# Block-transposed q features and 32x32 array tiles in the last stage of a linear-attention plus gMLP kernel

## The chip, the cores and the metric

The kernel runs on one core of one Trainium2 chip. The metric is the device time of one execution in microseconds; the kernel before takes 630.05 us, the median of three runs (629.80 to 630.59). A row of the profile names an engine: PE is TensorE's matmuls, PEld its weight loads, DVE VectorE, ACT ScalarE, POOL GpSimd, SP SyncE, which here only issues DMAs.

## What is computed

Both branches start from the same layer-normed input and are added to it (one batch, 2048 tokens, width 512, 32 heads of 16; gMLP width 1376, halved to 688):

```python
xn = layernorm(x)
# A: linear attention with learned features
q, k, v = split(xn @ wqkv)                          # per head: 2048 x 16
phi(t) = concat(softmax(t @ w_phi), softmax(-t @ w_phi))    # 32 features per head
kv = phi(k).T @ v                                   # per head 32 x 16
z  = sum_s phi(k)
o  = (phi(q) @ kv) / (phi(q) @ z + 1e-6)
A  = o @ wo
# B: gMLP
h = gelu(xn @ w_in);  z1, z2 = h[:, :688], layernorm(h[:, 688:])
g = w_sp @ z2 + b_sp[:, None]                       # over the 2048 tokens
B = (z1 * g) @ w_out
out = x + A + B
```

All tensors are fp32. Big products are done with operands split into a rounded part h and a remainder l (`fp32r`): `mm3` issues three matmuls, hh, hl, lh, at lines 55, 56 and 57. Other matmuls take plain fp32, and one of those stands as two records in the trace.

## The kernel before, in words

The 2048 tokens are 16 tiles of 128. The stages, in order of time:

1. To about 210 us: x is normed and transposed; per tile, v, k and q are projected, the features of k are summed into kv and z, the unnormalised features of q go to DRAM (`e_d`: 1024 exponentials and 64 reciprocals a token), z1 before its gelu too.
2. To about 282 us: the rest of z1; the gate weights' second half (`w2`, by `load_win`); z is broadcast (`make_zb`), kv is turned (`make_kvT`); the first spatial operands are prepared (`prep_a`); the features of q tiles 0 and 1 are finished by `q_fin` and stored to `e_d` again (lines 590 to 594); then z2 is projected, activated, normed and split into operands B for a Strassen-like product.
3. To 494 us: 32 steps of `products` for w_sp @ z2, two output tiles (a "pair") at a time in four steps; after each pair `drain` (lines 708 to 721) reads seven PSUM banks with VectorE, and `gate` forms u = z1 * g, which goes to DRAM in two 16-bit planes and comes back transposed by DMA.
4. The last stage, from 494 us: per pair of token tiles, u @ w_out (`project_u`, 17 matmuls of 512 columns a tile: five `mm3` and two for a rest of 48 rows), the attention, and o @ wo (`project_o`, 12 matmuls) accumulated into the same PSUM bank; VectorE adds x (line 944) and SP stores.

The attention of a pair before: `q_fin` (lines 490 to 501) finishes the features of a tile on VectorE: a product with z (L494), a sum per head half (L495), four small operations (L496 to L499), a scaling (L501). Then `attend_T` (line 887) transposes 16 blocks of 128x128 on TensorE against an identity and ScalarE copies them out of PSUM (L900) in four pieces; tiles from 6 on are first copied by a GpSimd DMA (L872) into an `fp32r` tile, which makes the transposes `fp32r`. `attend` (line 904) issues 16 matmuls with 64 rows, 32 columns and 256 tokens:

```python
lasts[3] = pe.matmul(po[r][c * QP:(c + 1) * QP, j // NG], kvT[rows, j], fs[j // 2][rows, j % 2],
                     start=True, stop=True).ins
```

ScalarE rounds the result (L47) and VectorE forms its remainder (L51). For u, `gated` joins the two planes on ScalarE (L774), rounds (L47) and lets VectorE take the remainder (L51, 128x640).

Order: a planner of the framework sets each engine's order by a simulated timeline, but `tc.issue_after(x)` pins what follows behind x. Before, a few such pins (`fin`, `lasts`) order the last stage. DMA queues of SP and POOL are in order as well: an issue that waits holds what stands behind it. The PSUM banks of the last stage are two pools, `pst` (5 banks: transposes and attention) and then `pso` (3 banks: outputs), laid over the 8 banks of the spatial products.

The gate of the last pair of rows (tiles 14 and 15) is done late, in the last stage, after tile 9 (line 998).

Of the kernel before, what the change touches and what calls it, by code (L numbers as in the profile page):

```python
# [10 lines left out]
F32 = mybir.dt.float32  # L11
# [8 lines left out]
P = 128  # L20
S, D, H, DH, FH = 2048, 512, 32, 16, 688
NT = S // P
# [17 lines left out]
def mixer(ctx: ExitStack, tc: tile.TileContext, x, x_t, wv, wqkT, phi_bd, wo, w_in, wst, b_r, w_out, out):  # L40
# [449 lines left out]
    def q_fin(et, tmp, zb):  # L490

        e, r, t, w = et[:, :NF], *(et[:, NF + k * 2 * H:NF + (k + 1) * 2 * H] for k in range(3))
        den = et[:, NF + 6 * H:QW]
        dve.tensor_tensor(tmp, e, zb, op=ALU.mult)  # L494
        dve.tensor_reduce(t, heads(tmp), axis=AX.X, op=ALU.add)  # L495
# [5 lines left out]
        return e, dve.tensor_tensor(heads(e), heads(e), bc(w, 2 * H), op=ALU.mult).ins  # L501
# [45 lines left out]
    NE = 2  # L547
    with ExitStack() as p1:
# [27 lines left out]
        with ExitStack() as p1a:  # L576
            ta = p1a.enter_context(left("tmp1a", 1))
            for j in range(2):
                load_win(w2[j], 2 + j, ta)
# [9 lines left out]
        tb = p1.enter_context(left("tmp1b", 1))  # L589
        for s in range(NE):  # L590
            et = load_q(s, tb.tile([P, QW], F32, tag="et", bufs=2, name="et"))
            tmp = zw.tile([P, 4, FC], F32, tag="z2", bufs=2, name="qtmp").rearrange("p a b -> p (a b)")[:, :NF]
            e, _ = q_fin(et, tmp, zb)
            sp.dma_start(e_d[s, :, :NF], e)
# [131 lines left out]
    def gate(i, cb, z, planes):  # L726
        cb, first, _ = cb
        with tc.issue_after(first):
            act.activation(z[:, :, :FH], z[:, :, :FH], AF.Gelu_apprx_tanh)
# [6 lines left out]
        dve.tensor_copy(z[:, :, rm], rh.bitcast(F32))  # L736
        planes = planes.bitcast(U16).rearrange("p (k two n) -> p k two n", k=2, two=2)
        for k in range(2):
            act.activation(planes[:, k], halves(z[:, k]), AF.Copy)
# [52 lines left out]
    lasts, wu = [None] * 6, []  # L792

    def first_q(s):
        e = slot("eq", F32R)[:, :NF]
        sp.dma_start(e.bitcast(F32), e_d[s, :, :NF])
        return e
# [12 lines left out]
    g, es, ets = {}, {}, {}  # L810
    for n in range(NC):
# [4 lines left out]
        if n % NQ == NQ - 1 and i < NP - 1:  # L816
            c = gt.tile([P, 2 * UP], F32, tag="c", name="c")
            gate(i, drain(i, g, c[:, :2 * FH].rearrange("p (a b) -> p a b", a=4)), z, c)
# [9 lines left out]
        if n == NC - 3:  # L828
            zs = slot("zb", F32R)
            zb, ident_r = zs[:, :NF].bitcast(F32), zs[:, NF:NF + P]  # L830
            round_h(act, ident_r, ident)
# [3 lines left out]
            ets[2] = load_q(2, slot("et"))  # L835
            q2 = slot("qtmp")[:, :NF]
        if n == NC - 2:
            u1t = load_u(1, slot("u1").bitcast(U16)[:, :2 * UP])
            es[0], es[1] = first_q(0), first_q(1)
            ets[3] = load_q(3, slot("et"))  # L840
            wo_raw = []
            for c in range(ND):
                rows = [(r, r + QP) for r in range((c % 2 * NG * 2 + c // 2) * QP, D, 2 * QP)][:NG]
                t = ws.tile([P, QC, P], F32, tag=f"f{c // 2}", bufs=2, name="wof").rearrange("p a b -> p (a b)")
                with tc.issue_after(load_q.last):
                    wo_raw.append(load_part((sp, pool)[c % 2], wo, rows, t))
# [3 lines left out]
    with tc.issue_after(lasts[1]):  # L850
        es[2], last = q_fin(ets.pop(2), q2, zb)
    mid.close()

# [5 lines left out]
    fin = []  # L859

    def fetch_u(i):
        return load_u(i, cw.tile([P, 2 * UP], U16, tag="u", bufs=3, name="ut"))

    def features(s):
        with tc.issue_after(fin[-1]):
            es[s], ins = q_fin(ets.pop(s), slot("qtmp")[:, :NF], zb)
        fin.append(ins)
        if s < PLAIN:
            return
        e = es[s]  # L870
        es[s] = cw.tile([P, NF], F32R, tag="er", bufs=5, name="er")
        features.copied = pool.dma_start(es[s].bitcast(F32), e).ins  # L872

    def gated(t):
        u = joined(t, cw.tile([P, UP], F32, tag="uj", bufs=2, name="uj"))
        return gate_parts(u, wk.tile([P, KF * P], F32R, tag="uh", name="uh"),
                          wk.tile([P, KF * P], F32R, tag="ul", name="ul"), wk.tile([2 * REM, P], F32R, tag="rt", name="rt"))

    kvT = cw.tile([P, 2 * NG, QP], F32, name="kvT")
    us = {}  # L880
    ctx_psg.__exit__(None, None, None)
    fin.append(last)
    sp.dma_start(kvT.rearrange("p j b -> p (j b)"), kvT_d)
    pst = ctx.enter_context(psum("pst", 5))
    pso = ctx.enter_context(psum("pso", 3))

    def attend_T(s):

        fs = []
        for g in range(NG):  # L890
            pt = pst.tile([P, 2, 2, P], F32, tag="tr", name="ptq")
            for a in range(2):
                for k in range(2):
                    src = group(es[s + k], 2 * g + a)
                    if src.dtype == F32:
                        pe.transpose(pt[:, a, k], src, ident)
                    else:
                        pe.transpose(pt[:, a, k].bitcast(F32R), src, ident_r)  # L898
            f = wk.tile([P, 2, 2 * P], F32, tag="f", bufs=NG + 1, name="f")
            attend_T.last = act.activation(f, pt.rearrange("p a k b -> p a (k b)"), AF.Copy).ins  # L900
            fs.append(f)
        return fs

    def attend(fs):

        oT = [wk.tile([P, NG, 2 * P], F32R, tag=f"oT{k}", name="oT") for k in "hl"]
        po = [pst.tile([P, 2, 2 * P], F32, tag="tr", name="po") for _ in range(2)]
        for j in range(2 * NG):
            c = j % NG
            for r in range(2):  # L910
                rows = slice(r * HP, (r + 1) * HP)
                lasts[3] = pe.matmul(po[r][c * QP:(c + 1) * QP, j // NG], kvT[rows, j], fs[j // 2][rows, j % 2],  # L912
                                     start=True, stop=True).ins
        for k in range(2):
            gs = slice(2 * k, 2 * k + 2)
            lasts[5] = round_h(act, oT[0][:, gs], po[k])
            ins = rest_l(oT[1][:, gs], po[k], oT[0][:, gs])
        return oT, ins

    def project_u(i, u, between=None):  # L920
        uh, ul, rt = u
        parts = [(slice(0, D), pso.tile([P, D], F32, tag="out", name="pout"))]
        if i == NT - 1:
            more = pst.tile([P, 4, P], F32, tag="tr", name="pout2").rearrange("p a b -> p (a b)")
            parts = [(slice(k * D // 2, (k + 1) * D // 2), q[:, :D // 2]) for k, q in enumerate((parts[0][1], more))]
        order = ExitStack()
        for ds, p in parts:
            for c in range(KF):
                i_ = mm3(p, (uh[:, c], ul[:, c]), tuple(w[:, ds] for w in wu[c]), c == 0, False)
                if between and c == KF // 2:  # L930
                    order.enter_context(between(i_))
            for w in wu[KF]:
# [103 lines left out]
```

## Time and profile before

| what | value |
|---|---|
| median of three runs | 630.05 us (629.80 to 630.59) |
| span of the profiled execution, first to last instruction | 628.4 us |
| PE busy | 622.3 us |
| DVE busy | 505.3 us |
| ACT busy | 313.5 us |
| granted TensorE clock, mean | 1.000 |
| DMA, mean | 180 GB/s |

The span is that of one profiled execution; the page gives no other time of it, and the runs are timed separately. In a row of a timeline stand start, duration, engine, line, operation, output <- inputs, shape and count; in brackets the idle time before it and what ended it. In a row of a group stand busy time, mean duration in ns, and idle time. Matmuls overlap, so their durations add up to more than the time they take.

### The profile page before, as it was taken

To read this page: it belongs to the slowest core of one execution; us is meant where nothing else is said; L and a number is where in the kernel's file an instruction comes from. 1 tells how busy PE (TensorE), PEld (TensorE's weight loads), DVE (VectorE), ACT (ScalarE), POOL (GpSimd) and SP (SyncE) were. 2 spreads that over 40 slices of the span, in tenths; PEclk is the share of its full clock that TensorE was granted. 3 is DMA by queue.
4 is the path that set the end of the run, shared out by engine and by line. 5 is a ranking of instruction groups with operands and counts; after the bars stand their busy time and mean duration, and the time that the engine had idled before them with its cause. 6 is when DMAs were issued, how large, how long until landed. Compare 5 with 4: busy or idle time off the path is not lost.

```text
span 628.4 us, 11487 instructions
## 1 busy us (share of the span) xinstructions
PE 622.3 (99%) x4375; PEld 563.1 (90%) x4375; DVE 505.3 (80%) x925; ACT 313.5 (50%) x463; POOL 121.0 (19%) x213
## 2 busy tenths in 40 slices
PE   9999999999999999999999999999999999999997
PEld 6888888888888999999999999999999878877776
DVE  5979989998988579989987677786777789989721
ACT  5623333432343447788553654546445655557550
POOL 4552232222101004552010110101101200110100
PEclk9999999999999999999999999999999999999999
DMA  8467767555653861001467758667588966897921
GB/s 326 152 160 163 200 176 162 166 157 151 165 164 106 265 211 68 2 1 57 138 173 186 221 176 203 202 184 226 165 197 297 287 227 230 268 278 263 293 83 35
DMA packets 67091, 112.85 MB, mean 180 GB/s; under 512 B 30588, under 2 KB 32124, under 8 KB 67036
## 3 DMA queue, kind: packets, MB, share of 16 engines
q1 hardware_dynamic: 53036, 63.35, 34.8%
q0 software_dynamic: 11408, 42.61, 23.8%
q10 hardware_dynamic: 2592, 6.16, 2.6%
q8 instruction: 34, 0.56, 0.4%
q14 instruction: 21, 0.17, 0.1%
HBM read 60.69 MB, written 31.48 MB: 147 GB/s over the span
## 4 chain that ended last, share of the span: by engine, by line
PE 96%; DVE 3%; issue 0%; ACT 0%
PE g L57 11%; PE g L56 11%; PE g L55 11%; PE proj L55 6%; PE zps L55 6%; PE proj L57 6%; PE proj L56 6%; PE zps L57 6%; PE zps L56 6%; PE pout L55 6%; PE pout L56 5%; PE pout L57 5%; PE po L912 1%; PE kvps L322 1%; PE ptq L898 1%; PE pout L933 1%
## 5 line engine op out<-in xcount | busy, mean ns | idle before, releaser
L55 PE MATMUL g<-B,A 128*128 128x344 f32 x448 | 143.2, 320 | 0.0
L56 PE MATMUL g<-B,A 128*128 128x344 f32 x448 | 143.2, 320 | 0.0
L57 PE MATMUL g<-B,A 128*128 128x344 f32 x448 | 143.0, 320 | 0.0
L57 PEld LDWEIGHTS g<-B,A 128*128 128x128 f32 x448 | 84.1, 188 | 0.2 <-DVE A L51 0.2
L56 PEld LDWEIGHTS g<-B,A 128*128 128x128 f32 x448 | 84.2, 188 | 0.0
L55 PEld LDWEIGHTS g<-B,A 128*128 128x128 f32 x448 | 84.2, 188 | 0.0
L47 ACT ACTIVATE A<-S 128x512 fp32r<-128x512 f32 x64 | 39.4, 628 | 63.3 <-DVE S L538 40.4
L116 ACT ACTIVATE e<-e,r_x 128x1024 f32<-128x1024 f32 x32 | 36.7, 1148 | 46.0 <-DVE e L115 44.1
L51 DVE TENSOR_TENSOR A<-S,A 128x512 fp32r<-128x512 f32 x64 | 43.1, 684 | 9.7 <-ACT A L47 9.6
L55 PE MATMUL proj<-wqk_h,xT 128*128 128x512 f32 x124 | 49.6, 400 | 0.0
L57 PE MATMUL proj<-wqk_h,xT 128*128 128x512 f32 x124 | 48.8, 394 | 0.0
L56 PE MATMUL proj<-wqk_l,xT 128*128 128x512 f32 x124 | 48.7, 393 | 0.0
L118 DVE TENSOR_REDUCE sm<-e 128x64 f32<-128x1024 f32 x32 | 38.6, 1210 | 9.7 <-ACT e L116 9.5
L47 ACT ACTIVATE A<-wf 128x512 fp32r<-128x512 f32 x64 | 33.0, 516 | 19.4 <-PE g L57 8.7
L51 DVE TENSOR_TENSOR A<-wf,A 128x512 fp32r<-128x512 f32 x64 | 35.2, 549 | 9.2 <-ACT A L47 9.0
L55 PE MATMUL zps<-w_h,xT 128*128 128x344 f32 x128 | 41.8, 326 | 0.4 <-ACT z1f L146 0.3
L57 PE MATMUL zps<-w_h,xT 128*128 128x344 f32 x128 | 40.9, 319 | 0.0
L56 PE MATMUL zps<-w_l,xT 128*128 128x344 f32 x128 | 40.8, 319 | 0.0
L537 DVE TENSOR_TENSOR S<-wf 128x256 f32<-128x256 f32 x32 | 13.4, 420 | 27.1 <-DMA wf<-in_wst 27.1
L146 ACT ACTIVATE z1f<-zps,r_x 128x344 f32<-128x344 f32 (+1 forms) x30 | 17.0, 565 | 33.8 <-PE zps L57 33.3
L302 ACT ACTIVATE v<-proj,r_x 128x512 f32<-128x512 f32 x16 | 11.0, 685 | 44.2 <-PE proj L57 41.7
L900 ACT ACTIVATE f<-ptq 128x512 f32<-128x512 f32 x32 | 16.5, 604 | 26.7 <-PE ptq L898 16.8
(199 smaller groups left out, 1546.4 us busy)
## 6 DMA issues: line engine op xcount, KB each, us to landing
wf<-in_wst SPq DMA_DIRECT2D x64, 256.0 KB, 3.9
e_d<-e POOLq DMA_DIRECT2D x16, 544.0 KB, 3.7
et<-e_d SPq DMA_DIRECT2D x16, 544.0 KB, 5.5
zacc<-e POOLq DMA_DIRECT2D x16, 512.0 KB, 4.9
z_d<-z1f ACTq DMA_DIRECT2D x16, 344.0 KB, 3.8
z1t<-z_d POOLq DMA_DIRECT2D x16, 344.0 KB, 5.8
u_d<-c POOLq DMA_DIRECT2D x14, 384.0 KB, 2.7
er<-et POOLq DMA_DIRECT2D x10, 512.0 KB, 4.9
```

The source lines that it names most:

```text
L47: return act.activation(h, src, AF.Copy).ins
L51: return (eng or dve).tensor_tensor(l, src, h.bitcast(F32), op=ALU.subtract).ins
L55: pe.matmul(dst, ah, bh, start=start, stop=False)
L56: pe.matmul(dst, ah, bl, start=False, stop=False)
L57: return pe.matmul(dst, al, bh, start=False, stop=stop).ins
L116: softmax_pair.exp = act.activation(e, e, AF.Exp, scale=scale).ins
L118: dve.tensor_reduce(sm, heads(e), axis=AX.X, op=ALU.add)
L146: z1_raw.last = act.activation(z[:, k], p, AF.Copy, scale=r_x[:, s:s + 1]).ins
L302: ins = act.activation(v[s], proj(s, wv_h, wv_l, rest_last), AF.Copy, scale=r_x[:, s:s + 1]).ins
L322: ins = pe.matmul(kv_acc[k:k + QP, m // 4], vs[:, m * QP:(m + 1) * QP], e[:, m * HP:(m + 1) * HP], start=s == 0 and m < 4, stop=s == NT - ...
L537: dve.tensor_tensor(sums[:, 0], b[:, 0], b[:, 1], op=ALU.add)
L900: attend_T.last = act.activation(f, pt.rearrange("p a k b -> p a (k b)"), AF.Copy).ins
```

## The change

Four things, all around the attention:

- **Features.** `q_fin` is cut into `q_weigh` (L494, L495), `q_norm` (the rest) and a new `q_turn`: one VectorE block transpose of 128x1024, which transposes each 32x32 block in place of its own. 32 columns are just the features of one head, so a block comes out with features on partitions and 32 tokens in a row. TensorE's transposes, their ScalarE copies and the DMA copies to `fp32r` are gone.
- **Attention.** `attend` handles four token tiles at once: 128 matmuls, each with 32 rows (one block of 32 tokens' features), 32 columns and 4 x 32 tokens, over all sixteen 32x32 parts of the array; each of the four row groups has its own PSUM bank. `kv4` holds kvT four times, one copy per row group, loaded from DRAM.
- **Early features.** Three tiles instead of two, ahead of the second gelu stage, written before the first `prep_a`, their loads at the stage's start; they are stored turned.
- **u remainders.** From tile 4 on, ScalarE writes -h and a GpSimd DMA adds u to it; tiles 2 and 3 keep VectorE.

Besides: everything in the last stage is pinned in written order per engine (`in_line`); `pso` (4 banks) is allocated before `pst` (4 banks); wo is loaded in whole row blocks and earlier; the features of tile 3 are weighed ahead of the last `drain`; the late gate stands before the third attention. The core of the diff:

```diff
+    def q_turn(et, eT):
+        return dve.transpose(eT, et[:, :NF]).ins
...
-    NE = 2
+    NE = 3
...
+            tb = p1a.enter_context(left("tmp1b", 1))
             ta = p1a.enter_context(left("tmp1a", 1))
+            def early_q(s):
+                ets[s] = load_q(s, tb.tile([P, QW], F32, tag="et", bufs=2, name="et"))
+            def early_features(s):
+                tmp = tb.tile([P, NF], F32, tag="tq", name="tq")
+                q_weigh(ets[s], tmp, zb)
+                q_norm(ets[s])
+                q_turn(ets.pop(s), tmp)
+                sp.dma_start(e_d[s, :, :NF], tmp)
+            early_q(0)
+            early_q(1)
             for j in range(2):
                 load_win(w2[j], 2 + j, ta)
...
             raw[0], raw[1] = load_a(0), load_a(1)
+            early_features(0)
+            for s in range(2, NE):
+                early_q(s)
+            for s in range(1, NE):
+                early_features(s)
             A[0] = prep_a(0, raw.pop(0))
...
+            with tc.issue_after(lasts[1]):
+                weigh(NE)
...
+    pso = ctx.enter_context(psum("pso", 4))
+    pst = ctx.enter_context(psum("pst", 4))
+    QT = 4
...
+    def features(s):
+        weigh_next(s)
+        normed_q(s)
+        turn_q(s)
+    def gated(i, on_dve=False):
...
+            round_h(act, uh, u[:, full])
+            line["act"] = act.activation(rt, u[:2 * REM, KF * P:], AF.Copy).ins
+            if on_dve:
+                line["dve"] = rest_l(ul, u[:, full], uh)
+            else:
+                line["act"] = act.activation(ul, uh.bitcast(F32), AF.Copy, scale=-1.0).ins
+                line["pool"] = pool.dma_start(ul.bitcast(F32), u[:, full], accum_op=ALU.add).ins
+    def attend(k):
+        eg = egs.pop(k)
+        oT = [cw.tile([P, NG, QT, P], F32R, tag=f"oT{n}", name="oT") for n in "hl"]
+        po = [pst.tile([P, NG, QT, SQ], F32, tag="po", name="po") for _ in range(P // SQ)]
+        with in_line():
+            for g in range(NG):
+                for a in range(2):
+                    for c in range(P // SQ):
+                        for i in range(P // SQ):
+                            rows = slice(i * SQ, (i + 1) * SQ)
+                            h = 8 * g + 2 * c + a
+                            pi = pe.matmul(po[i][c * SQ:(c + 1) * SQ, g], kv4[rows, h % 4, h // 4],
+                                           eg[rows, :, h * SQ:(h + 1) * SQ], start=a == 0, stop=a == 1,
+                                           skip_group_check=True).ins
+            for i in range(P // SQ):
+                h, l = (t[:, :, :, i * SQ:(i + 1) * SQ] for t in oT)
+                ai = round_h(act, h, po[i])
+                vi = rest_l(l, po[i], h)
...
+    project_u(0)
+    fetch_u(3)
+    fetch_u(4)
+    normed_q(NE)
+    project_u(1)
+    gated(2, True)
+    turn_q(NE)
+    project_u(2)
...
+    for k in range(NT // QT):
+        b = k * QT
+        if k == 2:
+            with in_line():
+                gate(NP - 1, cb, z)
...
+        oT = attend(k)
+        project_u(b + 3)
+        if k == 2:
+            with in_line():
+                store_gated(NP - 1, z, gt.tile([P, 2 * UP], F32, tag="pl", name="pl"))
...
+            fetch_u(NT - 2)
+        for i in range(b, b + QT):
+            last = i == b + QT - 1
+            fetch_q(i + 6)
+            if i == 0:
+                turn_q(QT)
+            elif i + 4 < NT and not last:
+                features(i + 4)
+            if i + 4 < NT and not last:
+                gated(i + 4)
+            project_o(i, oT)
+            if last and i + 4 < NT:
+                features(i + 4)
+                project_u(b + 4)
+                gated(i + 4)
...
+        if k < NT // QT - 1:
+            weigh_next(b + 2 * QT)
+            project_u(b + 5)
+            project_u(b + 6)
```

So between two attentions TensorE does, in this order, the u projection of the fourth tile of the block, the o projections of its four tiles, and the u projections of the first three tiles of the next block; VectorE does the remainders of the attention, the features of the next four tiles (the first is weighed beforehand), and four output sums.

More of the change, by code (lines that the diff above doesn't have):

```diff
@@ L588, in mixer @@
         sp.dma_start(zb_d, zb)
[L589 to L594, printed above, removed]
     ctx_w1.__exit__(None, None, None)
@@ L849, in mixer @@
         uT.append(first_gate(u1t, wu_rest[1]))
-    with tc.issue_after(lasts[1]):
-        es[2], last = q_fin(ets.pop(2), q2, zb)
+    line.update(act=lasts[0], dve=lasts[1])
     mid.close()
@@ L885, in mixer @@
[L885 to L918, printed above, removed]
@@ L920, in project_u, with in_line @@
-    def project_u(i, u, between=None):
-        uh, ul, rt = u
+    ctx_psg.__exit__(None, None, None)
+    pso = ctx.enter_context(psum("pso", 4))
+    pst = ctx.enter_context(psum("pst", 4))
+    QT = 4
+    full = slice(0, KF * P)
+    us, egs, nxt, p = {}, {}, {0: uT[0], 1: uT[1]}, {}
+    wo_h, wo_l = (cw.tile([P, ND, D], F32R, name=f"wo{k}") for k in "hl")
+    def in_line():
+        order = ExitStack()
+        for ins in line.values():
+            order.enter_context(tc.issue_after(ins))
+        return order
@@ L927, in project_u @@
[L927 to L932, printed above, removed]
-                lasts[2] = pe.matmul(p, rt, w[:, ds], start=False, stop=False).ins
-        order.close()
-        return parts
-    def project_o(i, oT, parts):
-        ts = slice(i % 2 * P, (i % 2 + 1) * P)
-        xr = wk.tile([P, D], F32, tag="xr", bufs=3, name="xr")
-        sp.dma_start(xr, x[i * P:(i + 1) * P, :])
-        for ds, p in parts:
-            for c in range(ND):
-                lasts[4] = mm3(p, (oT[0][:, c, ts], oT[1][:, c, ts]), (wo_h[:, c, ds], wo_l[:, c, ds]), False, c == ND - 1)
-            dve.tensor_tensor(xr[:, ds], p, xr[:, ds], op=ALU.add)
-            sp.dma_start(out[i * P:(i + 1) * P, ds], xr[:, ds])
@@ new lines, in project_u, with project_o @@
+        with in_line():
+            for ds, q in parts:
+                for c in range(KF):
+                    mm3(q, (uh[:, c], ul[:, c]), tuple(w[:, ds] for w in wu[c]), c == 0, False)
+                for w in wu[KF]:
+                    ins = pe.matmul(q, rt, w[:, ds], start=False, stop=False).ins
+        line["pe"] = ins
+        p[i] = parts
+    def project_o(i, oT):
+        xr = wk.tile([P, D], F32, tag="xr", bufs=4, name="xr")
+        sp.dma_start(xr, x[i * P:(i + 1) * P, :])
+        for ds, q in p.pop(i):
+            with in_line():
+                for c in range(ND):
+                    pi = mm3(q, (oT[0][:, c, i % QT], oT[1][:, c, i % QT]), (wo_h[:, c, ds], wo_l[:, c, ds]),
+                             False, c == ND - 1)
+                line["dve"] = dve.tensor_tensor(xr[:, ds], q, xr[:, ds], op=ALU.add).ins
+            line["pe"] = pi
+            sp.dma_start(out[i * P:(i + 1) * P, ds], xr[:, ds])
@@ new lines, in mixer @@
+    with in_line():
+        for c in range(ND):
+            ai, vi = split_w(wo_raw[c], wo_h[:, c], wo_l[:, c])
+    line.update(act=ai, dve=vi)
+    fetch_u(2)
+    for s in range(NE):
+        sp.dma_start(turned(s), e_d[s, :, :NF])
+    project_u(0)
[6 more added lines that the diff above has]
+    project_u(2)
+    fetch_u(5)
+    fetch_q(QT + 1)
+    with in_line():
+        weigh(QT)
+    gated(3, True)
+    fetch_u(6)
+    normed_q(QT)
```

165 lines of the change are left out of this document (66 added, 99 removed).

## The prediction, made before the result

> **What bounds the kernel now.** I read the page's busy shares first, then its 40 slices, then its chain that ended last.
>
> ```profile
> PE 622.3 (99%) x4375; PEld 563.1 (90%) x4375; DVE 505.3 (80%) x925; ACT 313.5 (50%) x463; POOL 121.0 (19%) x213
> ...
> PE   9999999999999999999999999999999999999997
> ...
> PE 96%; DVE 3%; issue 0%; ACT 0%
> ```
>
> TensorE (PE) is busy from the first slice to the last but one, and the chain is 96% TensorE. So time is won only by taking instructions away from TensorE, or by closing one of its few holes. The change lives in the last stage, after the spatial products; the busy time by stretch shows who has room there:
>
> ```profile
> 495.30:593.60 98.30, 98.30 (x648) 77.65 (x648) 90.47 (x143) 57.08 (x80) 7.71 (x15) 1.00 0.81 255
> 593.60:625.50 31.90, 31.43 (x232) 25.84 (x230) 7.14 (x11) 11.11 (x18) 0.00 (x0) 1.00 0.27 87
> ```
>
> The columns are PE, weight loads, VectorE (DVE), ScalarE, GpSimd. VectorE is at 90.5 of 98.3 us until 593.6, then nearly idle:
>
> ```profile
> 591.15 1.23 DVE L501 TENSOR_TENSOR et<-et 128x1024 f32<-128x1024 f32 x1
> ```
>
> ```profile
> 608.64 1.48 PE L898 MATMUL ptq<-zb,er 128*128 128x128 f32 x16
> ```
>
> The last features are done at 592.4, 16 us before the last transposes take them. The change spends just this reserve. The TensorE timeline of one pair of token tiles gives the prices:
>
> ```profile
> 544.55 0.39 PE L57 MATMUL pout<-woh,oT 128*128 128x512 f32 x1
> 544.79 1.48 PE L898 MATMUL ptq<-zb,er 128*128 128x128 f32 x16
> 546.10 0.46 PE L55 MATMUL pout<-wu,uh 128*128 128x512 f32 x1
> 546.40 0.39 PE L56 MATMUL pout<-wu,uh 128*128 128x512 f32 x1
> ...
> 549.42 0.40 PE L57 MATMUL pout<-wu,ul 128*128 128x512 f32 x1
> 549.65 0.63 PE L933 MATMUL pout<-wu,rt 96*128 96x512 f32 x2
> 550.21 1.09 PE L912 MATMUL po<-f,kvT 64*32 64x256 f32 x32
> 551.24 0.50 PE L55 MATMUL pout<-wu,uh 128*128 128x512 f32 x1
> 551.57 0.39 PE L56 MATMUL pout<-wu,uh 128*128 128x512 f32 x1
> ```
>
> Matmuls are pipelined, so I price by start to start, not by duration: 549.42 to 549.65 is 0.23 us for a matmul of 512 columns. There is one hole, where the last stage begins:
>
> ```profile
> 494.18 0.32 PE L57 MATMUL g<-B,A 128*128 128x344 f32 x1
> 495.26 0.47 PE L55 MATMUL pout<-wu,uh_ul 128*128 128x512 f32 x1 [0.76 <-DVE c L712]
> ```
>
> **TensorE, removed.** Sixteen transposes per pair take 544.79 to 546.10, 1.31 us, and the matmul behind them needs 0.30 instead of 0.23: 1.38. The attention takes 550.21 to 551.24, 1.03 us; it starts 0.10 after the matmuls ahead of it would have made room (549.65 + 2 x 0.23), and the one behind it takes 0.33: 1.23. Together 2.61 us per pair, 20.9 for eight. Two pairs have transposes of the slower kind, and one attention waited for its evictions one by one:
>
> ```profile
> 528.47 1.91 PE L896 MATMUL ptq<-ident,et 128*128 128x128 f32 x16
> 517.15 1.88 PE L912 MATMUL po<-f,kvT 64*32 64x256 f32 x32
> ```
>
> That is 1.91 - 1.48 = 0.4 twice and 1.88 - 1.09 = 0.8, so 22.5 us go.
>
> **TensorE, added.** Four attentions, each of 4 x 2 x 4 x 4 = 128 matmuls with 32 rows, 32 columns and a moving part of 128. The old one is 16 matmuls in the program and 32 in the trace, so the new one is 256 records. Before, eight parts of the array shared 32 records of 256 columns: 1024 columns each in 1.03 us. Now sixteen parts share 256 of 128: 2048 columns each, so 2.06 us if all sixteen run at once, and 2.26 with the 0.10 on each side. Four cost 9.0. This asks for a start every 2.06 / 256 = 8 ns, where the old one has 32 ns; the shortest that a group shows on its own is
>
> ```profile
> 11.99 2.09 PE L212 MATMUL fold<-bd,wrow 64*64 64x64 f32 x128
> ...
> 43.22 1.10 PE L322 MATMUL kvps<-e,v 128*32 128x64 f32 x64
> 44.25 0.50 PE L55 MATMUL proj<-wqk_h,xT 128*128 128x512 f32 x1
> ```
>
> ```profile
> L322 PE MATMUL kvps<-e,v x512: 219/219/244, 43.2 to 206.3; 128*32 128x64 f32 x171
> ```
>
> The 64 start every (1.10 - 0.22) / 63 = 14 ns, over four parts of the array; the 128 of L212 keep nearly that. By columns (16 of 64 per part, 1024 again, in 44.25 - 43.22 = 1.03 us) they use the array just as the old attention does, so 14 ns need be no floor of issue; but nothing here shows 8 ns either. I take 2.26 us and keep 3.8 (256 x 14 ns + 0.2) as the other end. [...]
>
> The hole of 495.26 - 494.34 = 0.9 us is a wait for the draining of a PSUM bank. The output tiles are now allocated ahead of the attention's, so the first takes another bank, one drained earlier; I book 0.9 gained, zero at worst. TensorE alone: 22.5 - 9.0 + 0.9 = 14.4 us less.
>
> **VectorE, the new cover.** It loses the u remainders of tiles 4 to 15 (they become a ScalarE copy and an adding DMA) and the features of tile 2, and gains thirteen transposes here.
>
> ```profile
> 531.54 1.22 DVE L494 TENSOR_TENSOR qtmp<-et,zb 128x1024 f32<-128x1024 f32 x1
> 536.33 1.22 DVE L494 TENSOR_TENSOR qtmp<-et,zb 128x1024 f32<-128x1024 f32 x1
> ...
> 592.29 1.28 DVE L944 TENSOR_TENSOR xr<-pout,xr 128x512 f32<-128x512 f32 x2
> ```
>
> ```profile
> L495 DVE TENSOR_REDUCE et<-qtmp 128x64 f32<-128x1024 f32 x14 | 17.0, 1214 | 0.2
> L51 DVE TENSOR_TENSOR ul<-uj,uh 128x640 fp32r<-128x640 f32 x14 | 11.2, 820 | 5.2 <-ACT uh L47 5.1
> L51 DVE TENSOR_TENSOR oT<-po,oT 128x512 fp32r<-128x512 f32 x16 | 10.4, 683 | 13.7 <-ACT oT L47 13.7
> L731 DVE TENSOR_TENSOR z1t<-z1t,c 128x1376 f32<-128x1376 f32 x1 | 1.6, 1584 | 0.0
> L47 ACT ACTIVATE oT<-po 128x512 fp32r<-128x512 f32 x16 | 8.7, 596 | 23.2 <-PE po L912 23.2
> ```
>
> ```profile
> L279 DVE STREAM_TRANSPOSE nmT<-nm_pad x11: 145/203/213, 29.4 to 141.1; 128x32 f32<-128x32 f32 x11
> ```
>
> Features of one tile, uninterrupted, are 536.33 - 531.54 = 4.79 us. A transpose of 1024 columns is not in the trace; that of 32 takes 203 ns. The reduction over 1024 with one input takes 1.21 us, about 1 ns a column and 0.15 fixed; if the transpose is such an operation it takes 1.2. From its own row alone it could need twice per column (203 is then 67 + 136 fixed): 2.3. I take 1.2, by the row of the same size, and keep 2.3. [...]
>
> So features now cost 6.0 a tile, and the four tiles of the next attention must be done when TensorE comes to it. Count both from E, the start of the matmul behind an attention. TensorE until the next: four u projections of 17 and four o projections of 12 matmuls, 116 x 0.23 = 26.7 us. VectorE, in the written order: first remainder at E + 0.8 (an eviction of 0.6 and the hand-overs); four at 0.64 (1.28 for two), 3.4; normalising (4.79 - 2.43 for its two first operations, done earlier), 5.8; transpose, 7.0; the first output sum, which waits for TensorE at E + 29 x 0.23 = 6.7 and a hand-over, 7.7; features 13.7; sum 14.3; features 20.3; two sums 21.6; features 27.6. VectorE is last by 1.0 us. In the third block the moved gate (1.6 us and three small ones, 2.2 in all) and the next weighing (2.4) lie between the last transpose and the remainders: 4.6 us where there are 3.1 (0.1 of hand-over, 2.2 of attention, 0.8), so 1.5 more. Waits: 1.0 + 1.0 + 2.5, and some 0.7 at the second and third u projection, whose remainders sit behind the split of wo and the normalising of tile 3. Together 5.2 us.
>
> **What moves at no cost.** The features of three tiles and three transposes now run ahead of the second gelu stage, 3 x 6.0 against 2 x 4.79, so 8.4 us more on VectorE. It idles there:
>
> ```profile
> 218.81 0.43 DVE L537 TENSOR_TENSOR S<-wf 128x256 f32<-128x256 f32 x1 [4.03 <-DMA wf<-in_wst]
> ...
> 229.81 1.23 DVE L494 TENSOR_TENSOR qtmp<-et,zb 128x1024 f32<-128x1024 f32 x1 [3.19 <-DMA et<-e_d]
> ```
>
> 7.2 us of the 8.4 fit into these two holes if the loads of q are early, as they are written now. What is left is worked off where VectorE waits for ScalarE, ahead of the last operands B of the products:
>
> ```profile
> 268.94 0.87 DVE L51 TENSOR_TENSOR B<-T,B 128x688 fp32r<-128x688 f32 x1 [1.75 <-ACT B L47]
> ...
> 283.41 0.87 DVE L51 TENSOR_TENSOR B<-T,B 128x688 fp32r<-128x688 f32 x1 [1.75 <-ACT B L47]
> ...
> 301.65 0.86 DVE L51 TENSOR_TENSOR B<-T,B 128x688 fp32r<-128x688 f32 x1
> ```
>
> From 283 to 302 it has no such wait, and TensorE, already in the products, follows close; so what is not absorbed by then is paid in full. I book nothing, and up to 8.4 us if the holes are not filled. The new stores of the turned features stand in SP's queue before its later loads, which have the same stage to land. The adding DMAs:
>
> ```profile
> zacc<-e POOLq DMA_DIRECT2D x16, 512.0 KB, 4.9
> ...
> u_d<-pl POOLq DMA_DIRECT2D x2, 384.0 KB, 5.4
> ```
>
> An adding DMA of 512 KB lands after 4.9 us; the new one has 320 KB and is issued at least 8 us (three o projections) before its u projection, behind its ScalarE copies. GpSimd loses ten copies of features for twelve of these. ScalarE loses 32 evictions of transposes. The wait in SP's queue for u of tile 14 (stored 5.4 us after its issue) has the third block's 23 us.
>
> **Sum.** 628.4 - 14.4 + 5.2 = 619.2 us of span. The page gives no other time of that execution; the median of the runs, 630.05, is 1.65 above its span, so the forecast is 620.9.
>
> **Rivals.** *A, the small matmuls come at the pace of L322.* 3.8 instead of 2.26 us, four times: +6.2, so 627.1. For it: no row shows anything closer. Against: those rows are explained by four parts and their columns.
>
> *B, slower: VectorE becomes the bound.* The place is the block transpose of the features, the price 2.3 us, as L279 read the other way. Then each block has four times 1.07 us more in the chain above, 4.3 a block, 12.8 in three, and 1 at tile 3: 634.7. It decides from about 1.9 us a transpose: (630.05 - 620.9) / 13 = 0.7 over 1.2. For it: L279 does not exclude it, and the stage has no reserve. Against: 145 ns, its shortest, would leave 78 ns fixed, half of the 0.15 us of L495.
>
> *C, a floor per matmul.* From 4 x (p x 0.256 + 0.2) = 9.0 + 9.2, a start every p = 17 ns eats all that the change gains; at 20 ns it is 633. For it: 256 matmuls in a row are twice the longest run here. Against: 14 ns in L322. [...]
>
> *D, late arrivals.* u remainders by DMA or the turned u of tile 14 reach TensorE late, 2 us in two blocks, or half of the 8.4 us of early features does: 625 either way. For it: the DMA share of 0.81, the longer chain to tile 14 (store, transposing load, join, adding DMA), the full VectorE from 283 to 302. Against: the margins above.
>
> **Chances.** Forecast 0.56; A 0.15; B 0.13; C 0.04; D 0.12. Without any VectorE wait it would be 615.7, and 0.3 per attention can be better: low end 614.5. A and D lie within 628; B and C, 0.17, are left out above it. What this kernel's measurement can tell from no change is about 0.2%, 1.3 us. Faster takes the forecast, D and nearly all of A, 0.81; same 0.04 (A and D together, and the near edge of B); slower 0.15.
>
> **What would show it.** Right: no transposes on PE in the last stage; four groups of 256 matmuls of 32x128, each about 2.1 us; VectorE transposes near 1.2 us; three waits of TensorE, ahead of the second to fourth attention, 1 to 2.5 us, released by VectorE's transpose; the last output sum at 616 instead of 625. Wrong: groups of 4 us (A) or more (C); transposes of 2 us and TensorE waiting 5 us per block (B); u projections released by a DMA (D); a hole of TensorE between 225 and 320 us, the early features.

## The result, and the profile after

The changed kernel takes 656.93 us, the median of four runs (653.46 to 660.35), against 629.93 us for the kernel before, the median of four too: a ratio of 1.042, 95% interval 1.038 to 1.046. It is slower by 27 us, where 9 us less had been forecast. The profiled execution has a span of 656.3 us. First the page of the kernel after: its busy shares, two of the rows in slices, and the chain that ended last.

```profile
span 656.3 us, 12727 instructions
...
PE 627.3 (96%) x5015; PEld 568.3 (87%) x5015; DVE 519.2 (79%) x929; ACT 308.2 (47%) x442; POOL 122.1 (19%) x209
...
PE   9999999999999999979999999999999697896987
...
PEclk9999999999999999989999999999999899697999
...
PE 67%; DVE 14%; issue 9%; DMA 5%; POOL 3%; ACT 1%; SPq 0%; DVEq 0%; POOLq 0%
```

TensorE was busy throughout before. Now its row dips in the 18th slice (near 285 us) and again and again from the 32nd on, the granted clock dips with it, and the chain holds 9% "issue": time in which an engine waited for nothing that the profile can name. TensorE's timeline of the first two attentions shows what that is.

```profile
515.52 3.47 PE L953 MATMUL po<-eg,kv 32*32 32x128 f32 x245
523.07 0.67 PE L953 MATMUL po<-eg,kv 32*32 32x128 f32 x11 [4.08 <-issue]
523.66 0.80 PE L55 MATMUL pout<-wu,uh 128*128 128x512 f32 x1
524.25 0.63 PE L56 MATMUL pout<-wu,uh 128*128 128x512 f32 x1
524.68 0.63 PE L57 MATMUL pout<-wu,ul 128*128 128x512 f32 x1
...
528.24 0.39 PE L57 MATMUL pout<-wu,ul 128*128 128x512 f32 x1
528.46 0.39 PE L55 MATMUL pout<-wu,uh 128*128 128x512 f32 x1
...
529.62 0.39 PE L55 MATMUL pout<-woh,oT 128*128 128x512 f32 x1
```

```profile
553.35 1.88 PE L953 MATMUL po<-eg,kv 32*32 32x128 f32 x127 [0.84 <-DVE eg L508]
559.90 2.81 PE L953 MATMUL po<-eg,kv 32*32 32x128 f32 x128 [4.66 <-issue]
563.62 0.37 PE L953 MATMUL po<-eg,kv 32*32 32x128 f32 x1 [0.92 <-issue]
563.92 0.79 PE L55 MATMUL pout<-wu,uh 128*128 128x512 f32 x1
```

The two attentions run 245 and 127 of their 256 small matmuls in a row, then TensorE stands still for more than four microseconds in the middle, waiting for no operand that the profile could name. Ahead of the second stands a wait of 0.84 us for the last transpose, and behind the first a u product whose matmuls start 0.43 us apart instead of 0.23 (524.25 to 524.68 against 528.24 to 528.46): half clock (0.50 granted from 523.66 to 527.67). The third and fourth attention, from the same view in narrower windows:

```profile
593.91 2.00 PE L953 MATMUL po<-eg,kv 32*32 32x128 f32 x137 [0.83 <-DVE eg L508]
600.45 2.74 PE L953 MATMUL po<-eg,kv 32*32 32x128 f32 x119 [4.54 <-issue]
...
603.12 0.80 PE L55 MATMUL pout<-wu,uh 128*128 128x512 f32 x1
```

```profile
632.34 2.19 PE L953 MATMUL po<-eg,kv 32*32 32x128 f32 x147 [0.83 <-DVE eg L508]
635.80 1.74 PE L953 MATMUL po<-eg,kv 32*32 32x128 f32 x109 [1.27 <-issue]
637.48 0.39 PE L55 MATMUL pout<-wu,uh 128*128 128x256 f32 x1
```

From first start to the start behind, the four take 8.1, 10.6, 9.2 and 5.1 us, 33.1 together. The group view of the page adds the standing up (busy, mean ns, then idle time ahead of the instructions):

```profile
L953 PE MATMUL po<-eg,kv 32*32 32x128 f32 x1024 | 17.9, 312 | 18.0 <-issue 15.5
```

The other part of the loss lies ahead of the last stage, which starts at 501.46 instead of 495.26 us although the hole there is closed. TensorE's waits between 264 and 290 us; the same query on the kernel before lists none:

```profile
PE g L55 <- ACT z L678: 3.4, 1, 3.4
PE zps L55 <- ACT z L678: 1.1, 1, 1.1
```

From the same time, the first step of the products on TensorE's timeline, as it goes on after the longer wait:

```profile
289.61 0.66 PE L55 MATMUL g<-B,A 128*128 128x344 f32 x1 [3.39 <-ACT z L678]
290.06 0.49 PE L56 MATMUL g<-B,A 128*128 128x344 f32 x1
290.35 0.49 PE L57 MATMUL g<-B,A 128*128 128x344 f32 x1
```

The last gelus come late, and when the matmuls go on they start 0.29 us apart instead of 0.16, until 295.8; the granted clock from 289.6 to there is 0.50, before 1.00.

### The profile page after: what moved, and what is told of

It is laid out like the page before. It is cut to its first block, busy times and chain, and to the rows that moved or that the text cites. A ratio compares the mean times of both kernels' runs of the same rounds, so it can differ in the third digit from the quotient of the medians.

```text
span 656.3 us, 12727 instructions
## 1 busy us (share of the span) xinstructions
PE 627.3 (96%) x5015; PEld 568.3 (87%) x5015; DVE 519.2 (79%) x929; ACT 308.2 (47%) x442; POOL 122.1 (19%) x209
## 4 chain that ended last, share of the span: by engine, by line
PE 67%; DVE 14%; issue 9%; DMA 5%; POOL 3%; ACT 1%; SPq 0%; DVEq 0%; POOLq 0%
PE g L55 10%; PE g L56 10%; PE g L57 10%; PE proj L55 6%; PE proj L57 6%; PE proj L56 6%; PE po L953 3%; PE zps L55 3%; PE zps L57 2%; PE zps L56 2%; PE pout L55 2%; PE pout L57 2%; PE pout L56 2%; DVE et L496 2%; DMA u<-uT_d 2%
## 5 line engine op out<-in xcount | busy, mean ns | idle before, releaser
L55 PE MATMUL g<-B,A 128*128 128x344 f32 x448 | 144.6, 323 | 3.4 <-ACT z L678 3.4
L56 PE MATMUL g<-B,A 128*128 128x344 f32 x448 | 144.5, 322 | 0.0
L57 PE MATMUL g<-B,A 128*128 128x344 f32 x448 | 144.4, 322 | 0.0
L55 PEld LDWEIGHTS g<-B,A 128*128 128x128 f32 x448 | 85.3, 190 | 3.7 <-ACT z L678 3.7
L56 PEld LDWEIGHTS g<-B,A 128*128 128x128 f32 x448 | 85.2, 190 | 0.0
L57 PEld LDWEIGHTS g<-B,A 128*128 128x128 f32 x448 | 85.2, 190 | 0.0
L55 PE MATMUL proj<-wqk_h,xT 128*128 128x512 f32 x124 | 49.6, 400 | 0.0
L57 PE MATMUL proj<-wqk_h,xT 128*128 128x512 f32 x124 | 48.8, 394 | 0.0
L56 PE MATMUL proj<-wqk_l,xT 128*128 128x512 f32 x124 | 48.7, 393 | 0.0
L47 ACT ACTIVATE A<-wf 128x512 fp32r<-128x512 f32 x64 | 33.1, 519 | 25.5 <-PE g L57 22.3
L55 PE MATMUL zps<-w_h,xT 128*128 128x344 f32 x128 | 41.4, 323 | 0.4 <-ACT z1f L146 0.3
L56 PE MATMUL zps<-w_l,xT 128*128 128x344 f32 x128 | 41.2, 322 | 0.0
L57 PE MATMUL zps<-w_h,xT 128*128 128x344 f32 x128 | 40.9, 319 | 0.0
L953 PE MATMUL po<-eg,kv 32*32 32x128 f32 x1024 | 17.9, 312 | 18.0 <-issue 15.5
L797 ACT ACTIVATE uj<-ut 128x1536 uint16<-128x1536 uint16 x14 | 27.3, 1952 | 13.1 <-DMA ul<-uj 8.7
L47 ACT ACTIVATE oT<-po 128x512 fp32r<-128x512 f32 x16 | 8.3, 604 | 51.3 <-PE po L953 51.3
```

What stands on the lines that cost most here:

```text
L47: return act.activation(h, src, AF.Copy).ins
L55: pe.matmul(dst, ah, bh, start=start, stop=False)
L56: pe.matmul(dst, ah, bl, start=False, stop=False)
L57: return pe.matmul(dst, al, bh, start=False, stop=stop).ins
L797: act.activation(halves(u), t.rearrange("p (two n) -> p two n", two=2), AF.Copy)
L953: pi = pe.matmul(po[i][c * SQ:(c + 1) * SQ, g], kv4[rows, h % 4, h // 4], eg[rows, :, h * SQ:(h + 1) * SQ], start=a == 0, stop=a == 1, ski ...
```

## The experiments

**Theory 1.** An attention's 512 instructions (256 matmuls, each with its weight load) leave TensorE faster than new ones arrive. The DMA view has a queue of the kind `instruction`, which the theory takes for TensorE's: 12 packets of 0.20 MB together in the last stage after, 7 of 0.11 MB before. With the 3036 matmuls and weight loads that the trace has there after, and 1756 before, that is 253 and 251 a packet. In the fourth attention after, two of them lie 26 slices of 0.13 us apart, 3.4 us. **Theory 2.** The early features delay the gelus. **Rivals** of theory 1: the array or the PSUM banks stall when sixteen parts run at once, or each small matmul has a floor; of theory 2: that delay is taken up later.

**e1 and e2: fewer instructions, then the old number on the same columns.**

```diff
+    def upper(t):
+        return t.bitcast(mybir.dt.bfloat16).rearrange("p a (b two) -> p a b two", two=2)[..., 1]
...
-                            pi = pe.matmul(po[i][c * SQ:(c + 1) * SQ, g], kv4[rows, h % 4, h // 4],
-                                           eg[rows, :, h * SQ:(h + 1) * SQ], start=a == 0, stop=a == 1,
+                            pi = pe.matmul(po[i][c * SQ:(c + 1) * SQ, g], upper(kv4)[rows, h % 4, h // 4],
+                                           upper(eg)[rows, :, h * SQ:(h + 1) * SQ], start=a == 0, stop=a == 1,
```

e2 loops besides over two halves of the four tiles, `po[i][..., g, t]` and `upper(eg)[rows, t, ...]`.

> The changed kernel, but its attention reads only the upper 16 bits of each feature and of each entry of kv (as bfloat16), so that one pass does what two did: 128 matmuls and 128 weight loads per attention instead of 256 and 256, into the same places of the same banks, sixteen parts at once as before. Theory 1 (TensorE's instructions come in blocks of 256, at best one block in about 3.45 us, as the twelve fetches of the last stage show): 256 instructions are one block, the buffer covers them, so the stalls of 4.35, 4.93, 4.83 us inside the attentions and the half clock after them go; last stage 151.4 us down to about 124, time about 630 (625 to 634). Rival (the array or the banks stall when sixteen parts run, or a floor of each matmul): stalls inside the attentions stay, at most halved with the number of matmuls; time 643 to 657.

> As e1_upper_halves, but each matmul cut into two of half the columns (64 instead of 128), with a weight load each: the same columns through the array, the same banks, and 512 instructions per attention again. Theory 1 (instruction blocks): the stalls are back, about 4 to 5 us in each attention, with half clock behind them; time 648 to 658. Rival (columns, the array or the banks set it): as e1_upper_halves, within 3 us.

e1 took 632.16 us and e2 644.47, a single time each. TensorE's timeline at an attention of e1:

```profile
550.52 1.27 PE L957 MATMUL po<-eg,kv 32*32 32x128 bf16 x128 [0.75 <-DVE eg L508]
551.72 0.50 PE L55 MATMUL pout<-wu,uh 128*128 128x512 f32 x1
```

and at the first and the second of e2:

```profile
515.91 2.22 PE L958 MATMUL po<-eg,kv 32*32 32x64 bf16 x246
522.88 0.31 PE L958 MATMUL po<-eg,kv 32*32 32x64 bf16 x10 [4.75 <-issue]
...
552.39 2.27 PE L958 MATMUL po<-eg,kv 32*32 32x64 bf16 x252 [0.59 <-DVE eg L508]
```

With 256 instructions no attention stands still. With 512 on the same columns and banks the first one does, after 246 records, almost as in the changed kernel (245), and the fourth does, for 2.30 us; the second and the third run 252 records through. So 512 instructions run dry in some attentions and not in others, which is why e2 is below theory 1's range. The rival is out: sixteen parts at once and the columns are the same in e1, which has no pause. The pace tells something too: 128 records in 1.27 us and 246 in 2.22, less the last one's own 0.22 and 0.19, are both 8.3 ns a record, with 128 columns or with 64. So the pace did not depend on the columns. The full attention goes at (1.88 - 0.29) / 126 = 12.6 ns.

**e11: a second doubling.** Four slices of 32 columns in place of two of 64.

> As e1_upper_halves, but each matmul cut into four of a quarter of the columns (32 instead of 128), with a weight load each: the same columns, 1024 instructions per attention (256 in e1, 512 in e2). Theory 1 (blocks of 256 instructions, one in about 3.45 us, one or two of them ahead): four blocks, 7 to 12 us for an attention in place of 1.2, part of it standing still in stretches of 1 to 5 us; with the half clock behind them 660 to 685. Rival (no blocks, each matmul has a floor of 8.4 ns as in e1's steady pace): 512 x 8.4 ns = 4.3 us, 3.1 us more in each attention, 642 to 647, and no stretch of over 1 us without a matmul.

675.94 us, within theory 1's range and far outside the rival's. TensorE's timeline of the first stretch of its second attention, and of the whole fourth one:

```profile
560.04 2.23 PE L958 MATMUL po<-eg,kv 32*32 32x32 bf16 x245 [0.53 <-DVE eg L508]
...
642.68 1.44 PE L958 MATMUL po<-eg,kv 32*32 32x32 bf16 x150
646.03 1.31 PE L958 MATMUL po<-eg,kv 32*32 32x32 bf16 x128 [1.92 <-issue]
649.76 1.35 PE L958 MATMUL po<-eg,kv 32*32 32x32 bf16 x128 [2.42 <-issue]
653.22 1.17 PE L958 MATMUL po<-eg,kv 32*32 32x32 bf16 x106 [2.10 <-issue]
```

After a first stretch (245 and 150 records), 128 matmuls with their loads, 256 instructions, come at a time, with about 2 us of standing between here and up to 4.8 in the other attentions. The DMA view of the last stage, first of e1 and then of e11, counts the packets:

```profile
q8 instruction: 8, 0.13, 0.4%
```

```profile
q8 instruction: 20, 0.33, 0.7%
```

4 x 768 = 3072 more instructions are 12 more packets: 256 each, the number that comes at a time in e11. So by these counts the queue is TensorE's. With 512 instructions of 4 to 6 ns (8.3 and 12.6 ns a record) the new ones came too late.

How the matmuls follow the packets shows best in e11's fourth attention, where they are nearly all that the DMA engines carry. The DMA view from 642 to 655 us, in 40 slices of 0.325 us:

```profile
GB/s 359 410 221 6 0 50 0 0 0 0 0 0 0 0 0 50 0 0 0 0 0 0 0 0 0 0 0 50 0 0 0 0 0 0 0 0 0 50 0 0
...
q8 instruction: 4, 0.07, 2.1%
```

The four slices of 50 GB/s, 16 KB each, are the four packets. The first three stand at 643.6, 646.9 and 650.8 us; the matmuls go on at 646.03, 649.76 and 653.22, each time 2 to 3 us behind a packet, and VectorE, ScalarE and GpSimd do nothing in between. So new packets come about 3.5 us apart, for 256 instructions that take 1.35. The profile itself has no name for this wait but "issue".

**e3: the early features alone, on the kernel before.**

```diff
+            early_q(0)
+            early_q(1)
             for j in range(2):
                 load_win(w2[j], 2 + j, ta)
...
+            early_features(0)
+            early_q(2)
+            early_features(1)
+            early_features(2)
             A[0] = prep_a(0, raw.pop(0))
...
-        for s in range(NE):
-            et = load_q(s, tb.tile([P, QW], F32, tag="et", bufs=2, name="et"))
...
-            e, _ = q_fin(et, tmp, zb)
-            sp.dma_start(e_d[s, :, :NF], e)
```

> The kernel before, with one part of the change: three tiles' features worked out ahead of the second gelu stage, with the 32x32 transposes, instead of two tiles' after the first planes (the third result and the transposed copies are stored and not used). Theory 2: TensorE waits for gelus there (1.3 us at 266, 3.6 us at 286, with 0.81 of the clock behind it), so the last product comes about 7.1 us later and so does the end: about 637 (634 to 640). Rival (that delay is taken up by waits later on, and only the last stage counts): 629 to 631.

637.16 us, ratio 1.0105 (1.0083 to 1.0128): +7.2 us. Its waits between 255 and 320 us have the same line:

```profile
PE g L55 <- ACT z L673: 3.4, 1, 3.4
```

Theory 2 is confirmed in size and place. How much of it the third tile, the transposes and the earlier place cost each, e3 does not separate.

**e4 and e5: the full attention in four groups** of 64 records. In e4 the groups stand six, six and five matmuls of the u product apart (not up to fourteen, as its expectation has it), the last one behind the product's end; in e5 three apart (`if c < 3: part(1 + c)`).

```diff
-        with in_line():
-            for g in range(NG):
+        def part(g):
+            with in_line():
...
+        part(0)
+        project_u(k * QT + 3, part)
...
+            for c in range(KF):
+                with in_line():
+                    line["pe"] = mm3(q, (uh[:, c], ul[:, c]), wu[c], c == 0, False)
+                if c in (1, 3):
+                    part(1 + c // 2)
...
+            part(3)
...
-        project_u(b + 3)
```

> The changed kernel with the same 512 instructions of each attention in four groups of 128, with 6 to 14 matmuls of the u product (about 250 ns each) between one group and the next; the evictions follow the last group. Theory 1 (instruction blocks): 128 instructions at a time fit what is buffered, and the blocks come while the long matmuls run: no stall over 1 us, no half clock, last stage about 124 to 128 us, time about 630 (626 to 636), the 7.1 us of the early features still in it. Rival (sixteen parts at once stall the array, or each small matmul has a floor): the stalls stay, time 645 to 657.

> As e4_attention_in_four, but the four groups stand after none, three, six and nine matmuls of the u product, so that its last eight (2 us) run while ScalarE empties the sums. In e4 the stalls inside the attentions were gone, yet each attention was followed by an empty 2.37 us (TensorE waits for the first evicted half) and by about eight matmuls at 427 instead of 227 ns (half clock, 1.6 us). Theory 1, completed (instruction blocks; every empty stretch over about 2 us is followed by half clock): both go, 4 x (2.1 + 1.6) = 15 us less than e4, about 641 (637 to 645). Rival (128 instructions every 1.75 us are as fast as the blocks can come, so the stalls are back): 647 to 657.

e4 took 656.92 us (1.044, 1.040 to 1.048), e5 657.42 (1.044, 1.040 to 1.049): both times miss what theory 1 had said. e4's lies where its rival put it, though the stalls that the rival reckoned with went; e5's lies 0.4 us above its rival's range. TensorE's waits in e4's last stage:

```profile
PE pout L55 <- ACT oT L47: 8.4, 4, 2.1
...
PE po L953 <- issue: 0.5, 1, 0.5
```

The standing inside the attentions did go, from 15.5 to 0.5 us, but the last group now stood right ahead of the output products, which wait for the evictions, four times 2.1 us. By the starts, the four attentions with these waits still take 26 us, against 33 in the changed kernel. The clock went down behind the first two, to 0.62 over 4.5 us and 0.66 from 565 to 570. By stretch, behind the first (the column after POOL is the granted clock):

```profile
527.50:532.00 4.50, 4.44 (x12) 3.23 (x13) 2.20 (x3) 4.47 (x6) 0.78 (x1) 0.62 0.26 87
```

The output products last 424, 419 and 424 ns on average (64 records each of L55, L56 and L57), 390, 390 and 389 in the changed kernel. That makes some 26 records of 0.63 us instead of 0.39, and the clock behind the first pause makes about 8: three pauses of the four, an estimate. So e4 does not bear out e5's expectation, in which half clock follows every empty stretch of over about 2 us.

e5 covers the evictions but sets the groups closer, and the waits move again:

```profile
PE po L953 <- issue: 4.9, 3, 2.3
PE pout L55 <- ACT uh_ul L47: 3.5, 1, 3.5
...
PE pout L57 <- DMA ul<-uj: 1.9, 1, 1.9
```

With less between the groups some of the standing is back, as the rival had it for this spacing, and two waits that had been hidden come out: u of tile 1 from ScalarE, and a remainder from its adding DMA. Both kernels have one thing in common. TensorE's timeline at a group of e4 that does not stall:

```profile
590.32 1.06 PE L953 MATMUL po<-eg,kv 32*32 32x128 f32 x64 [0.81 <-DVE eg L508]
591.31 0.50 PE L55 MATMUL pout<-wu,uh 128*128 128x512 f32 x1
```

It takes 1.0 us for its 64 records, so an attention of four tiles in four groups costs 4 us even with no pause, and in one go, at 12.6 ns a record, it would cost 3.4 (an estimate; no run has it). Before, two pairs took 2 x (1.31 + 1.03) = 4.7 us for transposes and attention. There was about one microsecond to win for four tiles.

**e6, e7, e9, e12, e10: the early features undone.** e6 and e9 have e1's short attention, e7 e5's, e12 the full one.

```diff
-    NE = 3
+    NE = 2
...
-            early_features(0)
-            for s in range(2, NE):
-                early_q(s)
-            for s in range(1, NE):
-                early_features(s)
             A[0] = prep_a(0, raw.pop(0))
...
+        for s in range(NE):
+            ets[s] = load_q(s, tb.tile([P, QW], F32, tag="et", bufs=2, name="et"))
...
+            q_norm(ets[s])
+            sp.dma_start(e_d[s, :, :NF], ets.pop(s)[:, :NF])
...
                 weigh(NE)
+                line["dve"] = q_norm(ets[NE])
+                weigh(NE + 1)
...
+    for i in range(NE + 1):
+        turn_q(i)
```

> As e1_upper_halves (attention from the upper 16 bits, 256 instructions), with the early features undone: two tiles' features after the first planes as before the change, not transposed there; the third and fourth tile's at the end of the products, and the transposes of the first four at the start of the last stage. Theory 2: the 7.1 us of the gelu stage come back; and e1's wait of 4.27 us for u of tile 1, with 24 matmuls at 427 ns behind it (together about 9 us), need not be there: 616 to 625. Rival (the moved VectorE work delays the first attention as much as it gained): 628 to 634.

> As e5_four_with_cover (the full attention), with the early features undone as in e6. Theory: e5 less 7.1 us, 634 (629 to 638): with no stall and no idle stretch left, the attention of four tiles costs 4 x 1.0 us against 2 x (1.32 + 1.02) us before, so there is next to nothing to gain. Rival (the change is worth its 13 us once the stalls are out): 616 to 624.

e6 took 632.47 us (ratio 1.0036, 1.0016 to 1.0056), e7 653.41 (1.037, 1.033 to 1.041): the rival's figure for e6, and for e7 nobody's. The products of e6 do end at 494.3 again, 7 us earlier, but what was saved is lost ahead of the first attention. TensorE's waits in its last stage:

```profile
PE pout L55 <- DVE c L720: 8.0, 1, 8.0
PE pout L57 <- DVE ul L51: 4.6, 1, 4.6
```

The drain of the last products stood on VectorE behind the features of the fourth tile, whose load had not landed; e7 waits at the same two places (3.7 us each), for an adding DMA (3.1) and for the transposes (2.4). In e9 and e12 the fourth tile is weighed behind the drain, the remainders of u of tiles 2 and 3 are moved, and the first attention stands inside the fourth u product.

> As e6_upper_halves_late_features, which lost 8.4 us at 494 (VectorE stood 4.1 us ahead of the drain of the last products, waiting for the fourth tile's features to land) and 5.0 us at 512 (the remainder of u of tile 2 behind the transposes). Here the fourth tile's features come after the drain, the remainders of u of tiles 2 and 3 ahead of the transposes, and the first attention stands inside the fourth u product. Theory 2, completed (the work of four tiles' features ahead of the first attention fits, if it doesn't stand ahead of what TensorE waits for): TensorE waits 4 us for u of tile 1 and 0 to 3 us for the features, the rest as in e1 from 529 on: 625 (620 to 629), below before. Rival (VectorE has no room for it anywhere): 630 to 636.

> As e9_upper_halves_reordered, with the full attention of the changed kernel (512 instructions). Theory 1: the attention's stalls and the half clock after them cost what they cost between the changed kernel and e1 (24.8 us), less some 3 us since the first attention stands inside a u product: 643 to 652. Rival (the early features were the larger part of the loss): 628 to 636.

e9, with the drain ahead of the fourth tile, took 630.97 us (1.002, 0.9996 to 1.004), no different from before, which is its rival's figure and not theory 2's; e12 655.37 (1.040, 1.037 to 1.042), 24.4 us more with nothing changed but the number of instructions and the bits they read, as between the changed kernel and e1 (24.8). Theory 1's size is thus found twice, though e12 came out above its range by 3 us. In e9 TensorE also stands 2.0 us for "issue" outside the attentions, at a matmul of L56 (0.5 in e1, at one of L57): 256 instructions in a row do not stall themselves, but may leave too few for what follows, a guess that no view shows. Of e6's two waits of 8.0 and 4.6 us one is left in e9:

```profile
PE pout L57 <- DVE ul L51: 4.7, 1, 4.7
```

It is the remainder of u of tile 3, behind the features of tile 3 on VectorE. e10 exchanged the two and took the first two transposes back ahead of the gelus:

> As e9_upper_halves_reordered, which lost 5.1 us at 507 (the remainder of u of tile 3 stood on VectorE behind the features of tile 3) and came to its first attention at 515. Here that remainder stands ahead of those features, and the transposes of the first two tiles (2.4 us) are done early again, behind the first planes, where the two tiles' features stood before the change. Theory 1 and 2: the attention of 256 instructions saves about 3 us for each four tiles against before (4.7 to 1.2, less the waits of VectorE), and the first attention comes 4 to 5 us earlier than in e9, so 624 to 629, a little below before; up to 2.4 us of it are lost if the early transposes delay the gelus. Rival (the group of four tiles makes a late start that no order mends): 630 to 633.

640.38 us (1.017, 1.015 to 1.020), outside both ranges. This kernel put the turned features into a buffer that the gelus need next. Its waits between 225 and 250 us:

```profile
ACT L667 <- DMA e_d<-qtmp: 15.6, 1, 15.6
PEld zps L55 <- ACT z L667: 5.2, 1, 5.2
```

ScalarE waited for the store, and TensorE for ScalarE. Apart from that its first attention starts 22.5 us into the last stage, in e9 21.9: the order did not bring it forward, so a group of four tiles starts late in each order tried.

**e8: the adding DMAs undone, on e1** (`on_dve=True` throughout).

> As e1_upper_halves, with the remainders of u computed by VectorE as before instead of by a copy of ScalarE and an adding DMA: twelve times 0.82 us more on VectorE, twelve copies fewer on ScalarE, twelve DMAs of 320 KB fewer. Theory (the adding DMAs neither cost nor bring anything while VectorE is not the bound): 632, within 3 us. Rival (VectorE is close to the bound, so the DMAs bring something): 635 to 642. Other rival (the DMAs' transfers delay the loads of u, the 4.27 us wait at 505 among them): 622 to 628.

638.15 us, 6 us above e1, in the range of the first rival: VectorE is close to the bound. Both are single times, and ten runs of e9 lie up to 7 us apart, so the size is uncertain. The waits of TensorE for the transposes rise from 2.9 us in e1 to

```profile
PE po L957 <- DVE eg L508: 7.0, 3, 2.4
```

So the adding DMAs seem to be worth their place. No version tried beats the kernel before.

## Why the prediction was wrong, point by point

**The step that failed: the price of the attention.** "I take 2.26 us and keep 3.8", "Four cost 9.0". The four took 33.1 us, 24.1 more. 15.5 of it is TensorE standing in their middle; 256 x (12.6 - 8.0) ns, four times, is 4.7 of pace; the rest, 3.9, is slow running and starting up behind the pauses (128 records in 2.81 us at 559.90, 127 in 1.88 at 553.35). Pace alone would have left the forecast at about 625.6 us, still faster than before; the standing decided. The text had seen that no row showed 8 ns and that "256 matmuls in a row are twice the longest run here", but it drew from that a slower pace only. The longest run of before, 128 records (L212), is 256 instructions with its loads and has no pause, and neither have e1's; the supply of instructions never entered as a resource that could run out. Rival A had the pace nearly right (14 ns) and rival C the idea that so many matmuls cost more than their columns, but neither had the standing.

**What follows from it, not booked at all:** half clock. Behind the first three attentions the u product takes 5.96 us (523.66 to 529.62), 6.29 and 5.52 by the starts, at a granted clock of 0.65, 0.61 and 0.70; undisturbed, in e1 behind its second attention, it takes 4.05. Over three that is 5.6 us. With the 24.1 this is the whole miss of the last stage: it took 151.4 us (501.46 to 652.9) where the prediction made it 121.7 (494.34 to 616).

**The second step that failed: "I book nothing"** for the early features. They cost 7.1 us at the last product in the changed kernel and 7.2 in e3. The bound of 8.4 was right, and so was the sign named for it, a hole of TensorE before 320 us. The two holes of VectorE did not take up 7.2 us: between 200 and 240 us VectorE's busy time rose by only 3.4 (28.1 to 31.5), and the remainder stood in front of the statistics that ScalarE needs between its gelus: its waits for the normalisation (`z` for `nb`, 200 to 292 us) rose from 7.8 to 13.2 us. Rival D had booked half.

**What held.** The transposes of 128x1024 take 1.24 us (1.2 forecast), so rival B, VectorE's price, falls. As the group view of the last stage has it:

```profile
L508 DVE STREAM_TRANSPOSE eg<-et 128x1024 f32<-128x1024 f32 x13 | 16.2, 1244 | 0.4
```

TensorE's waits for VectorE ahead of the attentions are 0.84, 0.83 and 0.83 us, where 1.0, 1.0 and 2.5 were forecast. The long attentions gave VectorE time, but with e1's short ones the waits are 0.75, 0.74 and 1.44, so the forecast was high in any case. The hole of 0.9 us is closed. That the adding DMAs cost nothing held for the changed kernel, where no wait of TensorE names them, and e8 has it that they bring some 6 us. In e5 and e7 one of them came late, by 1.9 and 3.1 us, as rival D had feared.

**What the sum would have been** with these two sizes right: 619.2 + 24.1 + 5.6 + 7.1 = 656.0 us of span; 656.3 was measured, so the smaller terms balance.

Open is why a run gets 245 records in the first attention and 127 in the second before it dries up, and why two attentions of e2 do not dry up at all. It may depend on where the blocks' edges fall, which no view shows.

## What to carry to other kernels

Count the instructions of a burst, weight loads included, not its columns alone: 256 in a row ran here without a pause, 512 paused in all four attentions of the changed kernel and in two of four in e2, and what was won in columns was lost to their supply. A pause of TensorE can cost more than its length: behind the first of 2.1 us in e4 the clock was 0.62 for 4.5 us, 1.7 us more, so that wait was worth 3.8 (an estimate); behind the 3.9 us in e1 it was 0.50 for 5.7. And when work is moved to an earlier stage, read how full that stage's engine is in front of the things TensorE waits for, not how much it idles in all.

## What the runs showed of the hardware that was not expected

Small matmuls (bf16) on sixteen parts start every 8.3 ns, with 128 or 64 columns (e1, e2), and every 8.4 with 32 (e11: 2.23 us for 245), where the shortest of before was 14 ns (L322).

Half clock can follow an idle stretch with no change of the work: in e1, whose attentions never stall, TensorE waits 3.9 us for u of tile 1, and in the stretch behind it (its columns as in the stretches of e4)

```profile
509.50:515.20 5.70, 5.70 (x14) 4.27 (x15) 5.56 (x11) 4.96 (x8) 0.00 (x0) 0.50 0.69 232
```

the granted clock is 0.50 for 5.7 us. Of e4's four pauses of 2.1 us the first two did it too (0.62 and 0.66 above), and a third by the estimate there. In the changed kernel the clock stayed at 1.00 behind the 0.84 us ahead of the second attention (553.3 to 555.3) and behind the 1.27 us in the fourth (637.4 to 642). Which pauses of about 2 us it follows stays open.
